# Last tiles of two batches side by side, loads in another order, and a new written-out order of steps, in an attention and Fourier-mixing kernel

## The chip, the cores and the metric

The kernel runs on one core of a Trainium2 chip. The metric is the device time of one execution in microseconds; runs of the same kernel are compared by their median. Engines are named as the profile names them: PE (TensorE), DVE (VectorE), ACT (ScalarE), POOL (GpSimd) and SP (SyncE, which here only issues DMAs). A "q" behind an engine's name is its issuing sequencer.

## The reference

There are 4 batches, 4 heads, 1088 positions and heads of 32, so d_model is 128. First comes a linear attention with a polynomial sketch, then a Fourier mix and a small network:

```python
a, b = x @ S1.T, x @ S2.T                 # r = 8 each
phi(x) = outer product of a and b         # 64 features
kv  = sum over s of phi(k) v ;  z = sum over s of phi(k)
att = phi(q) kv / (phi(q) z + 1e-6)       # heads side by side: 1088 x 128
u   = att + real(fft(fft(att, axis=seq), axis=d_model))
un  = (u - mean(u)) / sqrt(var(u) + 1e-6) # over d_model
out = u + relu(un @ w_ch1) @ w_ch2        # 128 -> 512 -> 128
```

## The kernel before

**Tiles.** 1088 rows of a batch are 8 full tiles of 128 rows and a rest of 64. The rests ("last tiles") of two batches share one tile of 128 partitions: `kes`, `ves` and `qes` hold them for k, v and q, with the first batch of a pair in partitions 0 to 63 and the second in 64 to 127. A pair's last tiles are loaded in pieces by `load_last` (L169, one load for each batch), `load_qe` (L186, two loads for each batch) and `load_q0` (L196, four loads of a single row for a pair).

**Chains and their letters.** The work is written as Python generators, one for each chain, and a string `ORDER` says in which order their steps are put down; a step lasts until the next `yield`. For batch b: `k` makes phi(k) and kv (transposes `ptrk` L378, copy `kT`, sketch products `pab` L387, `ak` and `kp` L395, the sums `pk` L409, `pkv` L420, copy `kvz`); `q` makes phi(q) transposed (`ptrq` L476, copy `qT`, `pq` L491, copies `qa`, products `qpT` L505); `v` copies v beside a column of ones (`vpad`, on POOL); `p` makes the attention's output (`pnd` L526, then `den`, `rec`, `x` on DVE, sums `xw` and `xf` on POOL); `z` is the sequence transform (`pz`, `pze`, and `zr` on POOL). `d` and `m` are the two halves of the network in a batch (`pT`, copy `uT`, `ph` L666, relu `ht` on ACT and DVE in turn, `po` L679, `ot` on DVE, output), and `D` and `M` the halves of u and its statistics (`pu`, `u`, `stats` on DVE, `mv` on POOL, `rstd` on ACT). `y`, `e`, `E` are the chains of a pair's last tiles: `y` transposes k's and q's last tile (`ptrE`), copies both (`eT`), multiplies (`pabE`, `ae`, `ep`) and transposes q's part back (`pqptE`, `qpTe`). `S` sets up constants and issues the loads of batch 0, `T` makes the tables of sines in four steps, `W` the weights, `L` issues the loads of one further batch.

**What sets the order.** There is no scheduler: each engine runs its instructions in the order in which `ORDER` puts them down, and waits on semaphores for what an instruction needs. The string `BANKS` says which of the eight PSUM banks each step takes; a step waits until the bank's last reader is done. Tiles in the pool `load` have three buffers. Loads and outputs go through SP's queue in the order written, but k's second half and k's last tiles for batch 0, which ACT issues. For batch 0 the queue order is half of k, half of q, q's last tiles, the other half of q, v, v's last tiles, q's single rows. Ten matmuls on zeros (`keep_warm`) stand at the start of PE.

Of the kernel before, what the change touches and what calls it, by code (L numbers as in the profile page):

```python
# [10 lines left out]
FP32 = mybir.dt.float32  # L11
# [20 lines left out]
def _back(ap, n):  # L32
# [7 lines left out]
S k0 T S k0 v0 q0 L k0 q0 q0 y0 q0 k0 q0 k0 q0 q0 y0 y0 k0 T k0 q0 q1 k1 k1 q1 k0 q0 y0  # L40
T k1 q0 k1 k1 q1 T q1 p0 p0 v1 L p0 q1 q1 p0 p0 k1 T p0 k1 q1 v2 q1 q2 q1 q2 k1 p0 q1 k2
k2 W y1 q2 p1 p0 p1 p1 p1 p1 p1 q2 y1 L p1 k2 q2 y1 z0 k3 z0 k3 v3 q3 z0 d0 q3 m0 q2 k2
q2 z0 k2 k2 k3 q2 k2 D0 z1 m0 q2 k3 q2 m0 d0 z1 y1 k3 z1 M0 d0 k2 m0 E0 e0 m0 q3 p2 M0
q3 k3 D0 E0 q3 M0 p2 p1 p2 p2 p2 q3 k3 q3 q3 p2 k3 m0 q3 m0 q3 d0 E0 z1 M1 p2 e0 D0 d0
d1 e0 p2 p3 p3 M1 p3 p3 p3 m1 p3 e0 p3 z2 e0 d0 m1 d0 m1 D1 z2 e0 e0 m1 d1 m1 D2 d1 d2
M1 p3 d1 m1 d2 D2 D1 d1 d2 z3 D1 z3 z2 m1 z2 d1 z3 d1 d2 d2 e1 E1 z3 M2 e1 E1 e1 e1 e1
d2 D2 m2 M2 d2 E1 e1 e1 M2 D3 m2 m2 m2 m2 M3 m3 m2 m3 D3 d3 M3 m2 D3 m3 m3 M3 m3 d3 d3
d3 d3 m3 m3 d3 m3 d3 d3
"""
BANKS = [  # L50
# [11 lines left out]
def kernel(  # L62
# [74 lines left out]
    s_n = const.tile([128, 4], FP32, name="s_n")  # L137
    tx = const.tile([128, NTAB], FP32, name="tx")
# [15 lines left out]
    xbz = [const.tile([128, DM], BF16, name=f"xbz{i}") for i in range(B)]  # L154
    kes = [const.tile([128, H, D], FP32, name=f"ke{i}") for i in range(2)]
# [13 lines left out]
    def load_last(eng, src, dst_e, b):  # L169
        p0 = E * (b % 2)  # L170
        eng.dma_start(
            dst_e[b // 2][p0 : p0 + E, :, :],
            bass.AP(tensor=src.tensor, offset=src.offset + (b * H * S + 1024) * D,
                    ap=[[D, E], [S * D, H], [1, D]]),
        )
# [10 lines left out]
    def load_qe(eng, b):  # L186

        for c in range(2):
            p0 = E * (b % 2) + 32 * c
            eng.dma_start(  # L190
                qes[b // 2][p0 : p0 + 32, :, :],
                bass.AP(tensor=q.tensor, offset=q.offset + (b * H * S + 256 + 544 * c) * D,
                        ap=[[D, 32], [S * D, H], [1, D]]),
            )

    def load_q0(eng, b):  # L196
        for c in range(2):
            p0 = E * (b % 2) + 32 * c
            eng.dma_start(
                qes[b // 2][p0 : p0 + 1, :, :],  # L200
                bass.AP(tensor=q.tensor, offset=q.offset + (b * H * S + 544 * c) * D,
                        ap=[[D, 1], [S * D, H], [1, D]]),
            )

    def loads(b):
        km[b] = load.tile([128, H, 8, D], FP32, name="km", tag="km")
        vm[b] = load.tile([128, H, 8, D], FP32, name="vm", tag="vm")
        qt[b] = load.tile([128, 2, H, 4, D], FP32, name="qt", tag="qt")
        if b == 0:
# [60 lines left out]
    def chain_start():  # L270
# [14 lines left out]
        for i in range(4):  # L285
            iota(s_f[32 * i : 32 * i + 32, 2:3], [[1, 1]], 256 + 544 * (i % 2), 1)
# [10 lines left out]
        for i, t_ in enumerate(vpads):  # L297
            nc.vector.memset(t_[:, 8, :, :], 0.0)
            nc.vector.memset(t_[:, 0:8, :, D : D + 1], 1.0)
            nc.vector.memset(t_[E * i : E * i + E, 8, :, D : D + 1], 1.0)  # L300
        for t_ in xbz:
            nc.vector.memset(t_[:], 0.0)
        for i in range(4):
            nc.vector.memset(s_f[32 * i : 32 * i + 1, 2:3], 544.0 * (i % 2))
        nc.vector.memset(kk[:, DM : DM + 1], 0.0)
        nc.vector.memset(kk[:, DM + 32 : DM + 33], 544.0)
        nc.vector.tensor_scalar(out=s_n[:, 0:3], in0=s_f[:, 0:3], scalar1=1.0 / S, scalar2=None,
# [63 lines left out]
    def chain_k(b):  # L371
# [32 lines left out]
        for hh in range(2):  # L404
            for t in range(NT):
                for h in (hh, hh + 2):
                    src = kp[:, h, t, :] if t < 8 else ep[:, 0, h, :]
# [19 lines left out]
    def chain_y(i):  # L427

        a = Y[i]
        eT = tT.tile([128, 2, 128], FP32, name="eT", tag="eT")  # L430
        ptr = bank("ptrE")
        nc.tensor.transpose(ptr[:, 0:128], kes[i][:, :, :], ident_f[:, :])
        nc.tensor.transpose(ptr[:, 128:256], qes[i][:, :, :], ident_f[:, :])
        nc.scalar.copy(eT[:, :, :], ptr[:, 0:256])
        yield
        pab = bank("pabE")
        for c in range(2):
            for j in range(2):
                nc.tensor.matmul(
                    pab[64 * j : 64 * j + 64, 64 * c : 64 * c + 64],  # L440
                    eT[:, c, 64 * j : 64 * j + 64], sblk[:, :, :], start=True, stop=True)
        a_e = abp.tile([128, 8, R], FP32, name="ae", tag="ae")
        nc.scalar.copy(a_e[:, :, :], _ap(pab, 0, 128, 0, [[16, 8], [1, R]]))
        yield
        ep = ppp.tile([128, 2, H, 64], FP32, name="ep", tag="ep", bufs=2)
        nc.vector.tensor_tensor(
            out=_ap(ep, 0, 128, 0, [[64, 8], [R, R], [1, R]]),
            in0=_ap(a_e, 0, 128, 0, [[R, 8], [1, R], [0, R]]),
            in1=_ap(pab, 0, 128, R, [[16, 8], [0, R], [1, R]]), op=MULT)
        a["ep"] = ep  # L450
        yield
        qpTe = qpTp.tile([128, 2, 128], FP32, name="qpTe", tag="qpTe")
        a["qpTe"] = qpTe
        pt = bank("pqptE")
        for pr in range(2):
            nc.tensor.transpose(pt[:, 128 * pr : 128 * pr + 128],
                                ep[:, 1, 2 * pr : 2 * pr + 2, :], ident_f[:, :])
        nc.scalar.copy(qpTe[:, :, :], pt[:, 0:256])
        yield

    def chain_v(b):
# [3 lines left out]
        r = slice(E * (b % 2), E * (b % 2) + E)  # L465
        nc.gpsimd.tensor_copy(vpad[r, 8, :, 0:D], ves[b // 2][r, :, :])
# [46 lines left out]
    def chain_p(b):  # L513
# [4 lines left out]
        for t0 in (0, 3, 6):  # L518
            pnd = bank("pnd")
            for t in range(t0, t0 + 3):  # L520
                for pr in range(2):
                    o = 132 * (t - t0) + 66 * pr
                    for j in range(2):
                        r = slice(64 * j, 64 * j + 64)
                        lhsT = qpT[:, t, pr, r] if t < 8 else Y[b // 2]["qpTe"][:, pr, r]
# [27 lines left out]
        r = slice(E * (b % 2), E * (b % 2) + E)  # L553
        nc.scalar.copy(xbz[b][r, :], x[r, 8, :])
# [5 lines left out]
    def chain_z(b):  # L560
# [30 lines left out]
        o = E * (b % 2)  # L591
        nc.scalar.copy(zes[b // 2][:, :, o : o + E], _ap(pze, 0, 128, 0, [[E, 2], [1, E]]))
# [7 lines left out]
    def chain_u(b, g):  # L600
# [22 lines left out]
        rstd = sp.tile([128, 4, 1], FP32, name="rstd", tag="rstd")  # L623
# [11 lines left out]
        nc.gpsimd.tensor_tensor(out=m, in0=m, in1=d, op=ADD)  # L635
        nc.scalar.activation(out=rstd[:, 0:nt, :], in_=m, func=ACT.Sqrt, bias=bias_eps[:, :],
# [5 lines left out]
    def chain_f(b, g):  # L642
# [53 lines left out]
        if g == 2:  # L696
            for j in range(4):
                o = out.offset + (2 * b * S + 544 * j) * DM
                nc.sync.dma_start(
                    bass.AP(tensor=out.tensor, offset=o + 257 * DM, ap=[[DM, 31], [1, DM]]),  # L700
                    ot[32 * j + 1 : 32 * j + 32, 0, :])
                nc.sync.dma_start(
                    bass.AP(tensor=out.tensor, offset=o, ap=[[DM, 1], [1, DM]]),
                    ot[32 * j : 32 * j + 1, 0, :])
# [20 lines left out]
    for b in range(2):  # L725
        chains[f"y{b}"] = (lambda b=b: chain_y(b))
        chains[f"e{b}"] = (lambda b=b: chain_f(b, 2))
# [40 lines left out]
```

## Time and profile before

| what | value |
|---|---|
| median of 3 runs | 99.22 us (98.99 to 100.25) |
| the profiled execution: time | 99.94 us |
| the profiled execution: span from first to last instruction | 97.2 us |
| mean granted TensorE clock | 0.993 |
| busy: PE, DVE, ACT, POOL | 83.0, 68.1, 62.3, 44.5 us |
| read from and written to device memory | 7.22 and 2.23 MB |

The span lies inside the profiled execution; 2.74 us are around it. Busy time of PE is modelled and counts overlapping matmuls once. In the views a row "line engine op out<-in xcount" is a group of like instructions, and brackets or "<-" name what ended the idle time before it.

### The profile page before, as it was taken

To read this page: it belongs to the slowest core of one execution; us is meant where nothing else is said; L and a number is where in the kernel's file an instruction comes from. 1 tells how busy PE (TensorE), PEld (TensorE's weight loads), DVE (VectorE), ACT (ScalarE), POOL (GpSimd) and SP (SyncE) were. 2 spreads that over 40 slices of the span, in tenths; PEclk is the share of its full clock that TensorE was granted. 3 is DMA by queue.
4 is the path that set the end of the run, shared out by engine and by line. 5 is a ranking of instruction groups with operands and counts; after the bars stand their busy time and mean duration, and the time that the engine had idled before them with its cause. 6 is when DMAs were issued, how large, how long until landed. Compare 5 with 4: busy or idle time off the path is not lost.

```text
span 97.2 us, 3683 instructions
## 1 busy us (share of the span) xinstructions
PE 83.0 (85%) x1486; PEld 63.8 (66%) x1486; DVE 68.1 (70%) x223; ACT 62.3 (64%) x154; POOL 44.5 (46%) x103
## 2 busy tenths in 40 slices
PE   5998548599899796899998998959999999999930
PEld 1357426497897365786986797849876789665630
DVE  5850567983997109990368698886986979599980
ACT  6008339476927985398289887786199987587700
POOL 7200050009930499999300058397389775506000
PEclk9999999999999999999999999999999999999997
DMA  2926729999446389600000000011003005130333
GB/s 37 260 51 143 233 37 282 254 338 283 67 117 163 86 251 210 195 8 0 10 0 7 0 7 0 7 47 61 0 7 117 18 0 169 56 109 24 114 103 113
DMA packets 15232, 9.67 MB, mean 100 GB/s; under 512 B 4080, under 2 KB 15088, under 8 KB 15216
## 3 DMA queue, kind: packets, MB, share of 16 engines
q1 hardware_dynamic: 14320, 9.12, 34.5%
q10 hardware_dynamic: 896, 0.34, 1.5%
q8 instruction: 11, 0.18, 0.8%
q14 instruction: 5, 0.04, 0.2%
HBM read 7.22 MB, written 2.23 MB: 97 GB/s over the span
## 4 chain that ended last, share of the span: by engine, by line
PE 33%; DMA 19%; DVE 16%; SPq 15%; issue 5%; POOL 5%; ACT 3%; DVEq 0%
DMA km<-in_k_dram 7%; PE ph L666 6%; SPq L181 6%; DMA vm<-in_v_dram 5%; DVE ot L687 5%; DMA qt<-in_q_dram 5%; PE pq L491 3%; PE pnd L526 3%; PE po L679 3%; DVE ht L671 3%; SPq L163 3%; PE pz L574 3%; DVE stats L625 3%; DVE qpT L505 2%; PE pab L387 2%
## 5 line engine op out<-in xcount | busy, mean ns | idle before, releaser
L505 DVE TENSOR_TENSOR qpT<-qa,pq 128x256 f32<-128x256 f32 x32 | 11.8, 417 | 6.3 <-ACT qa L498 6.3
L463 POOL COPY vpad<-vm 128x1024 f32<-128x1024 f32 x4 | 4.2, 1039 | 22.9 <-DMA vm<-in_v_dram 17.5
L395 DVE TENSOR_TENSOR kp<-ak,pab 128x1024 f32<-128x1024 f32 x8 | 9.6, 1216 | 6.1 <-ACT ak L391 4.3
L671 DVE TENSOR_SCALAR ht<-ph 128x512 bf16<-128x512 f32 (+1 forms) x20 | 11.6, 603 | 2.2 <-PE ph L666 2.2
L498 ACT COPY qa<-pq 128x256 f32<-128x256 f32 x32 | 10.2, 379 | 3.9 <-PE pq L491 3.4
L666 PE MATMUL ph<-uT,w_b 128*128 128x512 bf16 (+1 forms) x40 | 10.8, 347 | 1.6 <-DVE qpT L505 1.3
L549 POOL TENSOR_TENSOR xw<-x 128x512 f32<-128x512 f32 x8 | 10.0, 1272 | 2.4 <-PE pkv L420 1.5
L687 DVE SCALAR_TENSOR_TENSOR ot<-po,rstd,u 128x128 f32<-128x128 f32 x34 | 9.5, 345 | 1.6 <-DMA out_dram<-ot 1.0
L669 ACT ACTIVATE ht<-ph 128x512 bf16<-128x512 f32 (+1 forms) x20 | 10.1, 533 | 0.6 <-PE ph L666 0.5
L679 PE MATMUL po<-w_b,ht 128*128 128x128 bf16 x136 | 10.0, 220 | 0.5 <-ACT ht L669 0.2
L551 POOL TENSOR_TENSOR xf<-xw 128x512 bf16<-128x512 f32 x8 | 10.0, 1273 | 0.3
L631 POOL TENSOR_TENSOR mv<-stats 128x4 f32<-128x4 f32 (+1 forms) x10 | 2.0, 201 | 16.7 <-DVE stats L625 15.0
L679 PEld LDWEIGHTS <-ht 128*128 128x128 bf16 x136 | 8.2, 98 | 1.7 <-ACT ht L669 0.6
L491 PE MATMUL pq<-qT,sab 32*64 32x256 f32 x256 | 9.0, 387 | 0.4 <-DVE x L536 0.4
L526 PEld LDWEIGHTS pnd<-kvz,qpT 128*64 128x64 f32 x256 | 8.1, 137 | 1.6 <-issue 0.8
L526 PE MATMUL pnd<-kvz,qpT 128*64 128x66 f32 x256 | 8.8, 223 | 0.3 <-issue 0.3
L409 PE MATMUL pk<-kp,vpad 128*33 128x64 f32 x256 | 8.6, 219 | 0.0
L409 PEld LDWEIGHTS pk<-kp,vpad 128*33 128x33 f32 x256 | 7.8, 111 | 0.4 <-ACT uT L661 0.4
L381 ACT COPY kT<-ptrk 128x512 f32<-128x512 f32 x8 | 4.5, 596 | 5.3 <-PE ps L323 5.3
L536 DVE TENSOR_TENSOR x<-pnd,rec 128x384 f32<-128x384 f32 x12 | 6.7, 558 | 0.6
L625 DVE BATCH_NORM_STATS2 stats<-u 128x6 f32<-128x128 f32 x34 | 7.1, 278 | 0.0
L476 PE MATMUL ptrq<-ident_f,qt 128*128 128x128 f32 x32 | 4.9, 277 | 2.6 <-DMA qt<-in_q_dram 2.6
(144 smaller groups left out, 196.7 us busy)
## 6 DMA issues: line engine op xcount, KB each, us to landing
qt<-in_q_dram SPq DMA_DIRECT2D x16, 128.0 KB
vm<-in_v_dram SPq DMA_DIRECT2D x4, 512.0 KB
km<-in_k_dram SPq DMA_DIRECT2D x3, 512.0 KB
out_dram<-ot SPq DMA_DIRECT2D x6, 256.0 KB
w_f<-in_moe_w_ch_dram SPq DMA_DIRECT2D x2, 256.0 KB
out_dram<-ot SPq DMA_DIRECT2D x4, 128.0 KB
km<-in_k_dram SPq DMA_DIRECT2D x1, 256.0 KB
km<-in_k_dram ACTq DMA_DIRECT2D x1, 256.0 KB
```

The source lines that it names most:

```text
L409: nc.tensor.matmul(pk[p0 : p0 + D + 1, 64 * hh : 64 * hh + 64], vpad[:, t, h, :], src, start=(t == 0), stop=(t == NT - 1))
L491: nc.tensor.matmul(pq[t][64 * c : 64 * c + 64, 256 * ab : 256 * ab + 256], _ap(sab, 32 * r, 32, 64 * ab, [[1, 64]]), _ap(qT, 32 * r, 32, 5 ...
L498: nc.scalar.copy(qa[:, i, :], pq[i][:, 0:256])
L505: nc.vector.tensor_tensor(out=_ap(qpT, 0, 128, 1024 * g + 256 * (i % 2) + i // 2, [[128, 2], [512, 2], [2, 64]]), in0=_ap(qa, 0, 128, 256 ...
L526: nc.tensor.matmul(pnd[r, o : o + 66], lhsT, kv[:, pr, :, :], start=True, stop=True)
L549: nc.gpsimd.tensor_tensor(out=xw[:, i, :, :], in0=x[:, 0:4, :], in1=x[:, 4:8, :], op=f)
L625: nc.vector.bn_stats(stats[:, i, :], u[:, i, :])
L666: nc.tensor.matmul(ph[:, 0:n], w1_b[:, 128 * c : 128 * c + 128], uT[:, 0:n], start=True, stop=True)
L669: nc.scalar.activation(out=ht[:, c, 0:n], in_=ph[:, 0:n], func=ACT.Relu)
L671: nc.vector.tensor_relu(ht[:, c, 0:n], ph[:, 0:n])
L679: nc.tensor.matmul(po[:, (i - i0) * DM : (i - i0 + 1) * DM], ht[:, c, i * 128 : (i + 1) * 128], w2_b[:, c, :], start=(c == 0), stop=(c == 3))
L687: nc.vector.scalar_tensor_tensor(out=ot[:, i, :], in0=po[:, (i - i0) * DM : (i - i0 + 1) * DM], scalar=rstd[:, i, :], in1=u[:, i, :], op0= ...
```

## The change

Six things change.

1. A pair's last tiles lie interleaved: row r of the pair's first and second batch stand in partitions 2r and 2r+1. One `load_last` with a pattern over both batches then brings k's tile, one v's, two q's, and two the single rows of q. v's tile is multiplied by `par`, a column of 0 and 1 that keeps one batch of the two, `qpTes` holds zeros in the other batch's columns, and the outputs of a last tile go out in four DMAs for a pair instead of eight.
2. The loads stand in another order: k (in two halves), q, v, and then the last tiles of a pair; the single rows of q come with the second batch. ACT issues only S1 and S2.
3. q's last tile gets a chain of its own, `w`; `y` keeps k's. The body of both is `last_tile`.
4. In `D`, `M` and `E` the square root for `rstd` becomes a step of its own, so that it can be placed later than POOL's `mv`.
5. The constants follow: `par`, `s_n` for the interleaved rows, no zeroing of `xbz` and of the whole last tile of `vpad`.
6. `ORDER` and `BANKS` are replaced whole. The first two table steps now stand ahead of the first k step; before, the first stood behind it and the second after most of batch 0's steps.

```diff
-S k0 T S k0 v0 q0 L k0 q0 q0 y0 q0 k0 q0 k0 q0 q0 y0 y0 k0 T k0 q0 q1 k1 k1 q1 k0 q0 y0
-T k1 q0 k1 k1 q1 T q1 p0 p0 v1 L p0 q1 q1 p0 p0 k1 T p0 k1 q1 v2 q1 q2 q1 q2 k1 p0 q1 k2
...
+S T T k0 S k0 q0 k0 q0 q0 k0 y0 q0 L q0 k0 y0 v0 y0 q0 q0 k0 q0 k1 k1 L T q0 L k0 k1 k0
+q1 k1 q0 q1 w0 p0 q1 q1 k1 v1 q1 p0 p0 k1 T k1 w0 p0 k2 q2 q1 w0 k2 T k1 w0 q1 q1 p0 q1
+p0 v2 k2 p1 q1 k2 q2 y1 k2 W p0 q2 y1 p1 p1 y1 k2 p1 q2 p0 k2 p1 k3 k3 z0 q2 k2 w1 q2 z0
...
+    qpTes = [const.tile([128, 2, 128], FP32, name=f"qpTe{i}") for i in range(2)]
...
-    def load_last(eng, src, dst_e, b):
-        p0 = E * (b % 2)
+    def load_last(eng, src, dst, i, r0, n, p0):
         eng.dma_start(
-            dst_e[b // 2][p0 : p0 + E, :, :],
-            bass.AP(tensor=src.tensor, offset=src.offset + (b * H * S + 1024) * D,
-                    ap=[[D, E], [S * D, H], [1, D]]),
+            dst[p0 : p0 + 2 * n, :, :],
+            bass.AP(tensor=src.tensor, offset=src.offset + (2 * i * H * S + r0) * D,
+                    ap=[[D, n], [H * S * D, 2], [S * D, H], [1, D]]),
         )
...
+        load_rows8(nc.sync, k, km[b], b, 0, 2)
         if b == 0:
-            load_rows8(nc.sync, k, km[0], 0, 0, 2)
...
-            load_rows8(nc.scalar, k, km[0], 0, 2, 4)
-            for i in (0, 1):
-                load_last(nc.scalar, k, kes, i)
-        else:
-            load_rows8(nc.sync, k, km[b], b)
-            if b == 2:
-                for i in (2, 3):
-                    load_last(nc.sync, k, kes, i)
+        load_rows8(nc.sync, k, km[b], b, 2, 4)
         load_q(nc.sync, b, 0)
-        if b % 2 == 0:
-            for i in (b, b + 1):
-                load_qe(nc.sync, i)
         load_q(nc.sync, b, 1)
         load_rows8(nc.sync, v, vm[b], b)
         if b % 2 == 0:
-            for i in (b, b + 1):
-                load_last(nc.sync, v, ves, i)
-            for i in (b, b + 1):
-                load_q0(nc.sync, i)
+            load_last(nc.sync, k, kes[i], i, 1024, E, 0)
+            load_last(nc.sync, v, ves[i], i, 1024, E, 0)
+            for c in range(2):
+                load_last(nc.sync, q, qes[i], i, 256 + 544 * c, 32, 64 * c)
+        else:
+            for c in range(2):
+                load_last(nc.sync, q, qes[i], i, 544 * c, 1, 64 * c)
...
-            nc.vector.memset(t_[:, 8, :, :], 0.0)
...
-        for t_ in xbz:
+        for t_ in qpTes:
             nc.vector.memset(t_[:], 0.0)
...
+        nc.vector.tensor_scalar(out=odd_i[:, :], in0=odd_i[:, :], scalar1=1, scalar2=None, op0=AND)
+        nc.vector.tensor_copy(par[:, 1:2], odd_i[:, :])
...
+    def last_tile(src):
+        eT = tT.tile([128, 128], FP32, name="eT", tag="eT")
+        ptr = bank("ptrE")
+        nc.tensor.transpose(ptr[:, 0:128], src[:, :, :], ident_f[:, :])
+        nc.scalar.copy(eT[:, :], ptr[:, 0:128])
+        yield
+        pab = bank("pabE")
+        for j in range(2):
+            nc.tensor.matmul(
+                pab[64 * j : 64 * j + 64, 0:64],
+                eT[:, 64 * j : 64 * j + 64], sblk[:, :, :], start=True, stop=True)
+        a_e = abp.tile([128, 4, R], FP32, name="ae", tag="ae")
+        nc.scalar.copy(a_e[:, :, :], _ap(pab, 0, 128, 0, [[16, 4], [1, R]]))
+        yield
+        ep = ppp.tile([128, H, 64], FP32, name="ep", tag="ep", bufs=3)
+        nc.vector.tensor_tensor(
+            out=_ap(ep, 0, 128, 0, [[64, 4], [R, R], [1, R]]),
+            in0=_ap(a_e, 0, 128, 0, [[R, 4], [1, R], [0, R]]),
+            in1=_ap(pab, 0, 128, R, [[16, 4], [0, R], [1, R]]), op=MULT)
+        return ep
...
     def chain_y(i):
+        Y[i]["ep"] = yield from last_tile(kes[i])
+        yield
+
+    def chain_w(i):
+        ep = yield from last_tile(qes[i])
+        yield
         pt = bank("pqptE")
...
-        nc.scalar.copy(qpTe[:, :, :], pt[:, 0:256])
+        for j in range(2):
+            nc.scalar.copy(_ap(qpTes[j], 0, 128, j, [[128, 2], [2, 64]]),
+                           _ap(pt, 0, 128, j, [[128, 2], [2, 64]]))
...
-        r = slice(E * (b % 2), E * (b % 2) + E)
-        nc.gpsimd.tensor_copy(vpad[r, 8, :, 0:D], ves[b // 2][r, :, :])
+        nc.gpsimd.tensor_scalar(out=vpad[:, 8, :, 0:D], in0=ves[b // 2][:, :, :],
+                                scalar1=par[:, b % 2 : b % 2 + 1], scalar2=None, op0=MULT)
...
         nc.gpsimd.tensor_tensor(out=m, in0=m, in1=d, op=ADD)
+        yield
+        rstd = sp.tile([128, 4, 1], FP32, name="rstd", tag="rstd")
         nc.scalar.activation(out=rstd[:, 0:nt, :], in_=m, func=ACT.Sqrt, bias=bias_eps[:, :],
...
-            for j in range(4):
-                o = out.offset + (2 * b * S + 544 * j) * DM
+            for c in range(2):
+                for r0, n, p0 in ((257, 31, 2), (0, 1, 0)):
...
```

More of the change, by code (lines that the diff above doesn't have):

```diff
@@ L137 @@
     s_n = const.tile([128, 4], FP32, name="s_n")
+    odd_i = const.tile([128, 1], I32, name="odd_i")
+    par = const.tile([128, 2], FP32, name="par")
     tx = const.tile([128, NTAB], FP32, name="tx")
@@ L284, in chain_start @@
         iota(kk[:, DM + E : DM + 320], [[1, 2], [2, 128]], 1, 0)
-        for i in range(4):
-            iota(s_f[32 * i : 32 * i + 32, 2:3], [[1, 1]], 256 + 544 * (i % 2), 1)
+        nc.gpsimd.iota(odd_i[:, :], pattern=[[1, 1]], base=0, channel_multiplier=1)
+        iota(s_f[0:64, 2:3], [[1, 1]], 512, 1)
+        iota(s_f[64:128, 2:3], [[1, 1]], 1600, 1)
         iota(kk[:, DM + 320 :], [[1, 2], [2, 128]], 545, 0)
@@ L425, in chain_k, with chain_y @@
                            _ap(pkv, 64 * c, 64, 0, [[D + 1, 2], [1, D + 1]]))
-    def chain_y(i):
-        a = Y[i]
-        eT = tT.tile([128, 2, 128], FP32, name="eT", tag="eT")
+    def last_tile(src):
+        eT = tT.tile([128, 128], FP32, name="eT", tag="eT")
         ptr = bank("ptrE")
-        nc.tensor.transpose(ptr[:, 0:128], kes[i][:, :, :], ident_f[:, :])
-        nc.tensor.transpose(ptr[:, 128:256], qes[i][:, :, :], ident_f[:, :])
-        nc.scalar.copy(eT[:, :, :], ptr[:, 0:256])
+        nc.tensor.transpose(ptr[:, 0:128], src[:, :, :], ident_f[:, :])
+        nc.scalar.copy(eT[:, :], ptr[:, 0:128])
         yield
         pab = bank("pabE")
[L437 to L443, printed above, removed]
+        for j in range(2):
[4 more added lines that the diff above has]
+        nc.scalar.copy(a_e[:, :, :], _ap(pab, 0, 128, 0, [[16, 4], [1, R]]))
         yield
-        ep = ppp.tile([128, 2, H, 64], FP32, name="ep", tag="ep", bufs=2)
+        ep = ppp.tile([128, H, 64], FP32, name="ep", tag="ep", bufs=3)
         nc.vector.tensor_tensor(
[L447 to L450, printed above, removed]
+            out=_ap(ep, 0, 128, 0, [[64, 4], [R, R], [1, R]]),
+            in0=_ap(a_e, 0, 128, 0, [[R, 4], [1, R], [0, R]]),
+            in1=_ap(pab, 0, 128, R, [[16, 4], [0, R], [1, R]]), op=MULT)
+        return ep
+    def chain_y(i):
+        Y[i]["ep"] = yield from last_tile(kes[i])
         yield
-        qpTe = qpTp.tile([128, 2, 128], FP32, name="qpTe", tag="qpTe")
-        a["qpTe"] = qpTe
+    def chain_w(i):
+        ep = yield from last_tile(qes[i])
+        yield
         pt = bank("pqptE")
@@ L524, in chain_p @@
                         r = slice(64 * j, 64 * j + 64)
-                        lhsT = qpT[:, t, pr, r] if t < 8 else Y[b // 2]["qpTe"][:, pr, r]
+                        lhsT = qpT[:, t, pr, r] if t < 8 else qpTes[b % 2][:, pr, r]
                         nc.tensor.matmul(pnd[r, o : o + 66], lhsT, kv[:, pr, :, :],
@@ L552, in chain_p @@
                                     op=f)
-        r = slice(E * (b % 2), E * (b % 2) + E)
-        nc.scalar.copy(xbz[b][r, :], x[r, 8, :])
+        nc.scalar.copy(xbz[b][:, :], x[:, 8, :])
         yield
@@ L590, in chain_z @@
                         start=False, stop=(par == 1 and t == 1))
-        o = E * (b % 2)
-        nc.scalar.copy(zes[b // 2][:, :, o : o + E], _ap(pze, 0, 128, 0, [[E, 2], [1, E]]))
+        nc.scalar.copy(_ap(zes[b // 2], 0, 128, b % 2, [[128, 2], [2, E]]),
+                       _ap(pze, 0, 128, 0, [[E, 2], [1, E]]))
         yield
@@ L622, in chain_u @@
         mv = sp.tile([128, 3, 4], FP32, name="mv", tag="mv")
-        rstd = sp.tile([128, 4, 1], FP32, name="rstd", tag="rstd")
         for i in range(nt):
```

61 lines of the change are left out of this document (25 added, 36 removed), and 14 rows, old and new, of the table BANKS.

## The prediction

> **What bounds the kernel now.** I read the page first.
>
> ```profile
> span 97.2 us, 3683 instructions
> ...
> PE 83.0 (85%) x1486; PEld 63.8 (66%) x1486; DVE 68.1 (70%) x223; ACT 62.3 (64%) x154; POOL 44.5 (46%) x103
> ...
> PE   5998548599899796899998998959999999999930
> ...
> PE 33%; DMA 19%; DVE 16%; SPq 15%; issue 5%; POOL 5%; ACT 3%; DVEq 0%
> ```
>
> TensorE is the busiest engine, but its gaps lie in the first half, and in the chain that ended last a third of the span is DMA and its issuing on SP (19% + 15%). The busy time by stage says how much. I cut at 5.44 (first real transpose, after the ten warm-up matmuls), at 43.44 (first pT matmul, where the second half of the network starts), and at 93.41 (last matmul):
>
> ```profile
> 5.44:43.44 38.00, 31.29 (x656) 25.12 (x654) 24.45 (x55) 24.04 (x63) 16.67 (x23) 1.00 0.67 171
> 43.44:93.41 49.97, 47.48 (x828) 37.08 (x824) 38.48 (x128) 36.78 (x91) 25.53 (x65) 1.00 0.11 37
> 93.41:97.20 3.79, 0.00 (x0) 0.00 (x0) 1.11 (x5) 0.00 (x0) 0.00 (x0) 0.82 0.42 138
> ```
>
> The first numbers are length and PE busy. So the span is 5.44 + (31.29 work + 6.71 idle) + (47.48 + 2.49) + 3.79 = 97.2 us, and two thirds of the idle time is in the stage that loads. PE's timeline names most of those 6.71 us, in brackets:
>
> ```profile
> 10.87 0.63 PE L476 MATMUL ptrq<-ident_f,qt 128*128 128x128 f32 x4 [1.43 <-DMA qt<-in_q_dram]
> 14.03 0.30 PE L433 MATMUL ptrE<-ident_f,qe 128*128 128x128 f32 x1 [1.23 <-DMA qe<-in_q_dram]
> 19.56 0.63 PE L476 MATMUL ptrq<-ident_f,qt 128*128 128x128 f32 x4 [1.13 <-DMA qt<-in_q_dram]
> 34.21 0.30 PE L433 MATMUL ptrE<-ident_f,qe 128*128 128x128 f32 x1 [0.45 <-DMA qe<-in_q_dram]
> 39.27 0.39 PE L439 MATMUL pabE<-sblk,eT 128*64 128x64 f32 x6 [1.33 <-issue]
> ```
>
> The first four, 4.24 us, wait for loads; 0.46 more (pk after ep at 17.12) follows from the late qe. The load queue shows why:
>
> ```profile
> 2.64 4.08 SPq L190 DMA_DIRECT2D qe<-in_q_dram  x4
> 6.77 1.26 SPq L181 DMA_DIRECT2D qt<-in_q_dram  x2
> 8.08 0.60 SPq L163 DMA_DIRECT2D vm<-in_v_dram  x1
> 8.72 1.26 SPq L171 DMA_DIRECT2D ve<-in_v_dram  x2
> 10.03 2.62 SPq L199 DMA_DIRECT2D qe<-in_q_dram  x4
> 12.70 0.44 SPq L163 DMA_DIRECT2D km<-in_k_dram  x1
> ```
>
> Each issue takes some 0.65 us of SP, whatever it brings: four qe loads (64 KB in all) hold the second half of q until 6.77, four single rows (2 KB) cost 2.62 us, and k of the second batch goes out only at 12.70. In the program every load also waits for the one eight before it. The data path is not the limit, as stretches of the same load stage show (last numbers: DMA share, GB/s):
>
> ```profile
> 12.20:14.60 2.40, 1.17 (x34) 0.58 (x26) 1.59 (x3) 0.88 (x3) 1.27 (x2) 1.00 0.27 36
> 14.60:17.00 2.40, 2.06 (x72) 1.48 (x56) 1.76 (x5) 2.20 (x8) 0.00 (x0) 1.00 0.96 284
> 19.40:21.90 2.50, 2.34 (x20) 2.20 (x20) 2.10 (x4) 1.94 (x5) 0.00 (x0) 1.00 1.08 336
> 24.30:26.70 2.40, 2.11 (x70) 2.02 (x68) 2.33 (x5) 2.40 (x5) 2.20 (x7) 1.00 0.43 68
> ```
>
> Large loads run at 254 to 336 GB/s (I take 285); where last tiles and single rows are issued it is 36 to 68.
>
> **The change, part by part.**
>
> **Loads.** Ahead of k of the second batch stand 11 loads on SP instead of 16: 0.72 + 11 x 0.65 = 7.9 us instead of 12.70. Now the data path decides. k, q and v of batch 0 are 1.57 MB: from 1.9 us at 285 GB/s until 7.4. The last tiles of a pair keep their 128-byte pieces; 196 KB at 36 to 68 GB/s is 2.9 to 5.4 us; 3.8 taken, nearer the faster row since fewer issues thin it out: ke at 8.7, all at 11.2. Then 1.84 us for each 0.52 MB: k1 13.0, q1 14.9, v1 16.7, weights 18.5, k2 20.3, q2 22.1, v2 24.0, last tiles 27.8, the rest by 33.3 (now 41). When are they wanted? pab ends at 9.6 (9.45 now); then ptrq 0.45, pq 1.05, ptrE 0.25, a wait of 0.65 (below), pabE 0.3, a wait of 0.3, pq 1.05 and half of pk 1.0 make 14.6 for k1. Going on in PE's new order in the same way gives 17.7 for q1, 24 to 25 for k2 and q2, 30 for the second ke: no load is late. So 4.24 + 0.46 us of idle time go. If the path were slower, see the last rival.
>
> The Trainium skill ("DMA: Bandwidth & Descriptors", Specifications) says that transfers under 512 B stay below line rate. It speaks against this change: the pieces stay at 128 B, and now they stand in one block ahead of the next batch. The 36 to 68 GB/s above agree; if all of that were packets and not issuing, a pair would cost 5.4 us, and k1 would land at 14.6, just when it is wanted.
>
> **The front.** ACT no longer issues ke (6.03 to 7.42, which held the first kT copy to 7.46), but the first two sines now stand there (1.15 us, as at 16.13 to 17.28) and wait for DVE's angles, now done at 6.2. DVE's constants lose about 1.2 us (four xbz memsets 0.33, vpad 0.42, four single rows 0.42) and gain about 1.4 (two qpTe memsets at 0.27, by wdummy's row of the same size, and nine operations on a column or less at 0.07 to 0.1). kT comes 0.2 later: **+0.2**. Behind it wait sblk's products and all of batch 0.
>
> **Own steps and splits.** The k and q halves of the last tile are now apart: eT four copies of 128x128 at 0.26 (u's row) instead of two at 0.38, +0.3; ae two more at 0.2; qpTe four at 0.26 (its strided form is not in the trace: 0.26 to 0.38) instead of two at 0.38, +0.3; together +1.0 on ACT, which is idle for 14 of the 38 us. ep four at about 0.4 for two at 0.69: +0.2 on DVE. ve's copy becomes a product, 0.54 (center's row) for 0.29: +1.0 on POOL, which now waits 10.10 us for v. None is charged to the end; uncovered, they cost at most 2.2. Eight output issues fewer on SP: nothing, since SP waits there (27.7 us for its first). rstd as its own step frees ACT from some of its 5.1 us of waiting for POOL; it still waits for the same five small POOL operations, only placed later.
>
> **New waits in the first stage.** (1) pabE needs eT, which ACT copies behind two qa copies: 0.65, with pq's second half queued behind it on PE. (2) That pq needs banks that DVE frees after kp and two qpT: 0.3. (3) DVE now does the second tables (3.25 us, 17.55 to 20.8 before) ahead of batch 0's second qpT group, and batch 1's first pq takes a bank of it: 20.3 against 19.5, 0.8, with pnd, pk and the copies behind. (4) The 1.33 of "issue" has no releaser in the trace: 0 to 1.33, I take 0.65, the middle. With the front, 2.6 us instead of 6.71. Ends: 0.5 if ACT's and DVE's turns fall well, 6.7 if all comes back.
>
> **Second stage.** PE's new order puts 4.3 us of batch 2 and 3 (pab 0.93, pk 2.1, pq 1.05, pnd 0.75, pkv 0.17, less ptrq 0.44 and pze 0.27) ahead of the first pT. 43.2 us of PE remain there; DVE keeps 37.9 of its 39.6 (38.48 + 1.11; a qpT pair, 0.7, and an x group, 0.95, move ahead with them): 88% of PE's time instead of 83%. Less slack: 2.8 instead of 2.49. Ends: 0.5, and 6.2 if DVE keeps all its 11.5 us of gaps up to its last operation (37.9 + 11.5 - 43.2).
>
> **Sum.** 5.44 + 78.77 + 2.6 + 2.8 + 3.79 = 93.4 us of span, 3.8 less. The profiled execution took 99.94 us, 2.74 more than its span, and lies 0.72 above the median of 99.22. So the new median is 99.22 - 3.8 = **95.4 us**.
>
> **The rivals.**
>
> *PE packs better.* "Busy" holds hidden waits: 16 po matmuls take 1.06 us in mid-stage, but two late groups took 1.15 and 1.40 and the closing 32 took 2.60, so 0.09 + 0.34 + 0.48 = 0.9 us over. If these go and the stalls shrink from 5.4 to 3.5: 95.4 - 0.9 - 1.9 = 92.6. Against it: the closing group waits for ht on DVE and ACT, as it will again.
>
> The skill ("Perfetto Trace Analysis", Identifying the Most-Contended Engine) calls matmul busy time a poor measure and takes weight-load time instead: 37.08 of 49.97 us in the second stage. This speaks for that rival; by it 12.9 us would be room, not 2.5.
>
> *DVE takes over.* The gain of the first stage is given back: second-stage stalls of 6.2, so 95.4 + 3.4 = 98.8, no difference. For it: at 65.03 PE stood 1.00 us for qpT; normalisation, relu and outputs all queue on one in-order DVE. Against it: with later data DVE sat idle for 13.6 us in the first stage, and kept PE waiting little in the second.
>
> *The loads run no faster: slower than before.* All of a pair's last tiles now precede k of the next batch, so if the path, not the issuing, set the early pace, everything behind is late. Place: q2, wanted by PE at 29.97 in the old run, with 4.9 MB up to it. Turning point: 4.9 MB / (29.97 - 0.7) = 167 GB/s. At 150 q2 lands at 33.4, 3.4 us late: 99.2 + 3.4 = 102.6. For it: the load stage averages 171. Against: 284 and 336 in the rows above, with the dips where small loads are issued.
>
> **How the numbers follow.** Forecast 0.55; better packing 0.17; DVE 0.18; slow loads 0.10. A measurement here tells about 2%, 97.2 to 101.2. Faster: 0.55 + 0.17 = 0.72; the same 0.18; slower 0.10. The ends of the unknown stalls alone give 91.0 to 102.9; 92.5 to 99.0 leaves out the slow loads and about a tenth beside.
>
> **What would show it.** Right: no wait of PE for qt or qe over 0.3 us; k of batch 1 issued near 8 us and the last load landed by about 34; PE idle in front of the first pT under 3 us; the ends of the last matmul and the span still 3.8 apart. Wrong: a DMA row among PE's longest releasers (slow loads); more than 4 us of PE idle after the first pT (DVE); PE standing over 1 us for a bank behind DVE's tables.

## The result, and the profile after

| kernel | median | the kernel before beside it | ratio, 95% interval |
|---|---|---|---|
| changed | 90.92 us (90.52 to 92.69) | 99.73 us | 0.9125 [0.9039, 0.9211] |
| changed, again on a later chip | 91.81 us (90.56 to 92.79) | 99.41 us | 0.9194 [0.9126, 0.9261] |

Some executions of a kernel come out one to three per cent longer than its others; the medians are over all executions, and the ratios with an interval leave the long ones out.

The forecast was 95.4 us, 92.5 to 99.0. The sign was right; the gain, 8.8 us beside 3.8, is more than twice the forecast, and the time lies below the range. The profiled execution took 90.52 us, 1.82 more than its span. Its page, in the order of the lines shown of before:

```profile
span 88.7 us, 3662 instructions
...
PE 80.2 (90%) x1481; PEld 63.0 (71%) x1486; DVE 67.7 (76%) x223; ACT 62.3 (70%) x160; POOL 45.7 (52%) x102
...
PE   4998979999999999999999999999999999798700
...
PE 64%; DVE 21%; ACT 4%; DMA 3%; issue 2%; SPq 1%; DVEq 0%; ACTq 0%
```

PE has nines from slice 7 on where it had holes up to the middle, and in the chain that ended last DMA and SP's issuing fell from 19% + 15% to 3% + 1%: PE itself is the chain now. The stretches, cut as before at the first transpose, the first pT matmul and the last matmul:

```profile
5.11:40.94 35.83, 34.62 (x804) 28.36 (x802) 25.88 (x62) 26.24 (x74) 18.13 (x23) 1.00 0.68 181
40.94:84.08 43.14, 41.72 (x672) 33.14 (x674) 36.85 (x123) 34.57 (x84) 25.43 (x65) 1.00 0.12 42
84.08:88.70 4.62, 0.01 (x1) 0.00 (x0) 1.12 (x4) 0.00 (x0) 0.00 (x0) 0.78 0.33 115
```

So 5.11 + (34.62 work + 1.21 idle) + (41.72 + 1.42) + 4.62 = 88.7. Against the forecast span of 93.4: start -0.33, PE's work 76.34 instead of 78.77 (-2.43), first-stage stalls 1.21 instead of 2.6 (-1.39), second-stage stalls 1.42 instead of 2.8 (-1.38), tail 4.62 instead of 3.79 (+0.83). Together -4.7.

What is left of PE's brackets in the first stage is two rows, and none is a load:

```profile
7.68 1.34 PE L374 MATMUL pab<-sblk,kT 128*64 128x64 f32 x32 [0.44 <-ACT kT L368]
11.58 0.34 PE L423 MATMUL pabE<-sblk,eT 128*64 128x64 f32 x4 [0.67 <-ACT eT L419]
```

The load queue:

```profile
1.73 2.75 SPq L184 DMA_DIRECT2D qt<-in_q_dram  x4
...
6.51 1.29 SPq L174 DMA_DIRECT2D qe<-in_q_dram  x2
7.85 1.11 SPq L166 DMA_DIRECT2D km<-in_k_dram  x2
```

q goes out whole by 4.5 us, its last tiles in two issues instead of four, and k of the second batch at 7.85 instead of 12.70; the last load packet ends at 33.1.

### The profile page after: what moved, and what is told of

The parts are those of the page before. It is cut to its first block, busy times and chain, and to the rows that moved or that the text cites. A ratio compares the mean times of both kernels' runs of the same rounds, so it can differ in the third digit from the quotient of the medians.

```text
span 88.7 us, 3662 instructions
## 1 busy us (share of the span) xinstructions
PE 80.2 (90%) x1481; PEld 63.0 (71%) x1486; DVE 67.7 (76%) x223; ACT 62.3 (70%) x160; POOL 45.7 (52%) x102
## 4 chain that ended last, share of the span: by engine, by line
PE 64%; DVE 21%; ACT 4%; DMA 3%; issue 2%; SPq 1%; DVEq 0%; ACTq 0%
PE pnd L518 11%; PE pq L483 10%; PE pk L396 10%; DVE ot L679 6%; DVE ht L663 5%; PE pab L374 5%; DVE stats L615 4%; PE ptrq L468 4%; PE ptrk L365 3%; DMA out_dram<-ot 3%; PE ph L658 3%; PE pz L565 3%; PE po L671 2%; PE pT L650 2%; PE pz L558 2%
## 5 line engine op out<-in xcount | busy, mean ns | idle before, releaser
L671 PE MATMUL po<-w_b,ht 128*128 128x128 bf16 x136 | 9.4, 219 | 0.4 <-ACT ht L661 0.4
L518 PE MATMUL pnd<-kvz,qpT 128*64 128x66 f32 x256 | 9.4, 224 | 0.0
L610 ACT COPY u<-pu 128x512 f32<-128x512 f32 (+1 forms) x10 | 5.3, 526 | 2.2 <-PE pu L605 0.8
L483 PEld LDWEIGHTS pq<-qT,sab 32*64 32x64 f32 x256 | 4.9, 131 | 2.3 <-PE ptrE L418 0.8
```

What stands on the lines that cost most here:

```text
L483: nc.tensor.matmul(pq[t][64 * c : 64 * c + 64, 256 * ab : 256 * ab + 256], _ap(sab, 32 * r, 32, 64 * ab, [[1, 64]]), _ap(qT, 32 * r, 32, 5 ...
L518: nc.tensor.matmul(pnd[r, o : o + 66], lhsT, kv[:, pr, :, :], start=True, stop=True)
L671: nc.tensor.matmul(po[:, (i - i0) * DM : (i - i0 + 1) * DM], ht[:, c, i * 128 : (i + 1) * 128], w2_b[:, c, :], start=(c == 0), stop=(c == 3))
```

## The experiments

The medians, each beside the kernel before on the same chip. "Joint" and "own" say whether the square root for rstd follows POOL's mv in the same step or is a step of its own. All runs but e6 and e13 keep the interleaved layout of the last tiles, with its constants and its four output DMAs for a pair.

| run | loads of last tiles | order of steps | rstd | median | before |
|---|---|---|---|---|---|
| e1 | few, new places | old | joint | 100.38 | 99.89 |
| e2 | many, old places | new | own | 94.17 | 99.89 |
| e3 | as changed, second sines late | new | own | 90.66 | 99.89 |
| e4 | as changed | new | joint, early | 104.63 | 99.89 |
| e5 | few, old places | old | joint | 95.26 | 99.51 |
| e6 | many, old places | old | own | 100.03 | 99.51 |
| e10 | many, new places | new | own | 94.93 | 99.51 |
| e11 | few, old places | new | own | 91.86 | 99.51 |
| e9 | as changed | new | joint, late | 104.88 | 99.41 |
| e8 | as changed, 3 output buffers | new | own | 89.77 | 99.41 |
| e12 | the changed kernel again | new | own | 91.81 | 99.41 |
| e13 | the kernel before, warm-up cut small | old | joint | 97.43 (one run) | 99.41 |

**New loads under the old order (e1).** All of the new loads and constants; `ORDER`, `BANKS`, the joint chain `y` and the joint square root as before.

```diff
-S T T k0 S k0 q0 k0 q0 q0 k0 y0 q0 L ...
+S k0 T S k0 v0 q0 L k0 q0 q0 y0 q0 k0 ...
-    def chain_w(i):
```

> The loads, the interleaved layout and its constants as in the changed kernel; ORDER, BANKS, the joint chain for k's and q's last tile and the joint rstd step as before. Theory A (the loads held PE, the new order only follows them): PE's four waits for loads and the wait for ep go, 4.7 us in brackets and some 0.17 us of drained pipeline with each, the other waits stay: span 91 to 92.5 us, PE idle in front of the first pT under 2.5 us. Theory B (the order is what holds PE; early data find it waiting for ACT and DVE instead): span 94 us or more, with new waits of PE for ACT or DVE ahead of the first pT.

Ratio 1.0104 [0.9991, 1.0218]. One row of PE's timeline tells why:

```profile
16.72 0.45 PE L420 MATMUL ptrE<-ident_f,qe 128*128 128x128 f32 x1 [5.71 <-DMA qe<-in_q_dram]
```

The joint chain transposes q's last tile right after k's, and q's single rows, which belong to that tile, now come with batch 1's loads. What the few loads gave went into that one wait. Neither theory has this: the time is theory B's, but the wait is for a load. So q's own chain is no tidying: under the old order, with the joint chain, the new places of the loads gain nothing.

**Few loads in the old places, old order (e5).** To keep e1's collision out, the few loads stand where the many stood.

```diff
+        if b % 2 == 0:
+            load_last(nc.sync, k, kes[i], i, 1024, E, 0)
         load_q(nc.sync, b, 0)
+        if b % 2 == 0:
+            for c in range(2):
+                load_last(nc.sync, q, qes[i], i, 256 + 544 * c, 32, 64 * c)
         load_q(nc.sync, b, 1)
         load_rows8(nc.sync, v, vm[b], b)
+        if b % 2 == 0:
+            load_last(nc.sync, v, ves[i], i, 1024, E, 0)
+            for c in range(2):
+                load_last(nc.sync, q, qes[i], i, 544 * c, 1, 64 * c)
```

> The kernel before, with its old order of steps, its joint chain for both last tiles and its joint rstd, but with the interleaved last tiles brought by few loads, which stand where the old loads stood in the queue (single rows of q ahead of batch 1's k, not with batch 1 as in the first run). Theory (the issuing of many small loads made PE wait for q): q's second half is issued near 4.9 us instead of 6.77, q's last tiles 1.3 to 2 us earlier, batch 1's k near 8 instead of 12.70; the stalls of 1.43, 1.23, 1.13 and 0.45 us go or shrink to under 1 us in all, the stages behind them start some 3 to 4 us earlier, and the ratio to before is 0.955 to 0.975 (95 to 97 us). Rival (the old order was fitted to the late loads, so the stalls only change their place): PE idle stays over 7.5 us in all and the ratio is 0.985 or more.

95.26 against 99.51 us: 4.25 us less, ratio of the medians 0.957, what the first theory said. The size is loose: the seven times of the kernel before run from 97.51 to 100.77, and its two shortest (97.51 and 98.5) beside the three shortest here (94.71 to 95.38) give 2.9 us. (The profile is of an execution of 96.86 us, so of its rows mainly the releasers are used.) PE's timeline:

```profile
12.10 1.12 PE L478 MATMUL pq<-qT,sab 32*64 32x256 f32 x32 [0.73 <-DVE qpT L492]
14.96 0.31 PE L396 MATMUL pk<-ep,vpad 128*33 128x64 f32 x4 [0.46 <-DVE ep L433]
20.15 0.44 PE L441 MATMUL pqptE<-ident_f,ep 128*128 128x128 f32 x2 [1.65 <-DVE qpT L492]
...
36.17 0.39 PE L426 MATMUL pabE<-sblk,eT 128*64 128x64 f32 x6 [0.93 <-issue]
...
61.94 0.45 PE L652 MATMUL ph<-uT,w_b 128*128 128x128 bf16 x2 [0.99 <-DVE qpT L492]
```

No load is among the releasers. What remains is the stall without a releaser, and PE behind DVE, in three of these rows for a tile that the matmul doesn't read, so for the bank; none of these rows is left in the changed kernel. This is what the order is worth. The last was there in the kernel before too, with one more of its kind:

```profile
60.77 1.12 PE L491 MATMUL pq<-qT,sab 32*64 32x256 f32 x32 [0.36 <-DVE x L536]
65.03 0.45 PE L666 MATMUL ph<-uT,w_b 128*128 128x128 bf16 x2 [1.00 <-DVE qpT L505]
```

**Old loads under the new order (e2).** The changed kernel with as many loads as before, in the old places and on the old engines; ACT issues k's.

```diff
-            load_last(nc.sync, k, kes[i], i, 1024, E, 0)
+            for h in range(2):
+                load_last(nc.scalar, k, kes[i], i, 1024 + 32 * h, 32, 64 * h)
...
```

> The changed kernel with the loads as before in number, order and issuing engine (k's second half and k's last tiles of the first pair on ACT, two to four small loads for each last tile, four single rows), in the interleaved layout. Theory A: the new order wants k and q of batch 1 at 14 and 18 us, and they land at 16 to 21, so PE waits for DMA 4 to 7 us in sum ahead of the first pT: span 93 to 96 us. Theory B: the order finds other work, waits for DMA stay under 2 us: span below 91 us.

94.17 us, 0.9493 [0.9389, 0.9597]. PE's timeline:

```profile
8.95 1.34 PE L383 MATMUL pab<-sblk,kT 128*64 128x64 f32 x32 [1.75 <-ACT kT L377]
11.29 1.09 PE L477 MATMUL ptrq<-ident_f,qt 128*128 128x128 f32 x4 [0.99 <-DMA qt<-in_q_dram]
```

Both stalls are the loads' doing: ACT is held by issuing ke (and now also by the first sines), and q's second half is late. They are 2.3 us more than the 0.44 in the changed kernel, of the 2.4 to 3.3 us between the medians. Neither theory holds whole: PE waits for loads under 2 us, as B said, but the span is 92.6, not under 91. The order alone, on the old loads, is worth some 5 us by the ratio (4.0 to 6.1), 5.7 by the medians.

**As many loads as before, in the new places (e10); few loads in the old places (e11).** Both under the new order.

e10 cuts every load of a last tile in two; e11's queue is that of e5.

```diff
-            load_last(nc.sync, v, ves[i], i, 1024, E, 0)
+            for h in range(2):
+                load_last(nc.sync, v, ves[i], i, 1024 + 32 * h, 32, 64 * h)
...
```

```diff
         load_rows8(nc.sync, k, km[b], b, 2, 4)
+        if b % 2 == 0:
+            load_last(nc.sync, k, kes[i], i, 1024, E, 0)
         load_q(nc.sync, b, 0)
...
```

> The changed kernel with every load of a last tile cut in two (k, v, q's tiles and q's single rows: 6 more issues for a pair ahead of or in batch 1's loads, 12 in all), same bytes, same pieces of 128 bytes, same order. Theory (the issues, 0.65 us each on one queue, set the pace of the early loads): batch 1's k is issued near 10.5 us instead of 7.85, which its transpose at 14.3 still forgives, but q's single rows go out near 18.5 instead of 14.5 and PE, which wants them at 18.5, waits 1 to 2.5 us for them; 92 to 93.5 us, ratio 0.925 to 0.945. Rival (the packets, not the issues, decide): landing times and the time stay as in the changed kernel, 90.5 to 91.3 us.

> The changed kernel, few loads and new order of steps, but the few loads stand in the queue where the old ones stood: k's last tiles ahead of q, q's last tiles between q's halves, and q's single rows ahead of batch 1's k. Theory (the number of issues matters more than their order): q's second half is issued 2 us later than in the changed kernel and PE waits 0.3 to 1.2 us for it at its first transposes; all else is in time: 91 to 92.2 us. Rival (order of need carries what the loads bring): PE waits 2 us or more for q, and the time comes near the 94.17 us of the changed kernel with the old loads.

e10 took 94.93 us, 3 to 4 more than the changed kernel, and more than either theory said; e11 91.86, level with the upper of the changed kernel's two medians (no changed kernel ran beside these two). So under the new order the number of issues carries the loads' part, and their places are worth under 1 us. The wait of 0.3 to 1.2 us for q that e11's theory named did not come; no load is among its releasers. The first theory of e10 had the sign but not the place: q's single rows went out late, and PE stood 0.87 us at their transpose (the profile names a bank behind DVE there), yet the longest wait was for q of batch 2, which all the issues ahead push back to 21.15 us, where the changed kernel has it at 16.34 (PE's timeline, e10):

```profile
27.13 0.63 PE L474 MATMUL ptrq<-ident_f,qt 128*128 128x128 f32 x4 [1.47 <-DMA qt<-in_q_dram]
```

**The square root: own step or joint (e4, e9, e6).** e4 puts it back behind mv in the early step; e9 moves statistics, mv and square root together to the late step; e6 gives the kernel before an own step at the head of the next.

```diff
         nc.gpsimd.tensor_tensor(out=m, in0=m, in1=d, op=ADD)
-        yield
         rstd = sp.tile([128, 4, 1], FP32, name="rstd", tag="rstd")
         nc.scalar.activation(out=rstd[:, 0:nt, :], in_=m, func=ACT.Sqrt, bias=bias_eps[:, :],
                              scale=1.0 / DM)
+        yield
```

```diff
+        yield
         stats = sp.tile([128, 4, 6], FP32, name="stats", tag="stats")
...
-        yield
         rstd = sp.tile([128, 4, 1], FP32, name="rstd", tag="rstd")
```

```diff
+        yield
         nc.scalar.activation(out=rstd[:, 0:nt, :], in_=m, func=ACT.Sqrt, bias=bias_eps[:, :],
                              scale=1.0 / DM)
-        yield
         nc.vector.reciprocal(rstd[:, 0:nt, :], rstd[:, 0:nt, :])
```

> The changed kernel with the square root for rstd back in the step of the statistics, so that ACT's queue stands for POOL as before; order otherwise the same. If the own step is worth something, ACT's waits for POOL grow from 2.2 us to 5 us or more and the span by 0.5 to 2 us. If ACT has room in the second stage (34.6 of 43.1 us busy), the span stays within 0.3 us.

> The changed kernel, but the statistics (bn_stats on DVE, mv on POOL) are moved behind the new yield as well, so that statistics, mv and the square root all stand together at the later place that the order gives to the square root. Theory (what counts is the distance between POOL's mv and the square root on ACT, in which ACT does other things): ACT waits for POOL 10 us or more again and the time is 100 us or more, like the run with the joint step at the early place (104.6). Rival (the joint step was only too early for ACT in that order; a late place is enough): 91 to 94 us.

> The kernel before, with one edit: the square root for rstd stands at the head of the following step, behind whatever the order puts in between, and not behind the statistics in the same step. Loads and the order of everything else as before. Theory (the square root ahead of other ACT work costs only where the order packs ACT tightly): ACT's 5.1 us of waiting for POOL shrink to under 3, but PE's idle time in the second half was only 2.49 us, so the ratio is 0.985 to 1.01. Rival (the own step is worth several us by itself): ratio under 0.975, with the 1.00 and 0.36 us stalls of PE in the second half gone.

104.63 (1.046 [1.0273, 1.0647]), 104.88 (1.0549 [1.0454, 1.0644]) and 100.03 us. ACT's waits (total, times, longest), first of the changed kernel, then of e4; e9 has 14.9 us in 8:

```profile
ACT rstd L628 <- POOL mv L625: 2.2, 3, 1.3
```

```profile
ACT rstd L627 <- POOL mv L625: 13.6, 10, 2.3
```

Early or late, a square root that stands right behind mv stops ACT, and with it copies and relus that PE waits for, as in this row of e4's PE timeline:

```profile
50.94 1.38 PE L483 MATMUL pq<-qT,sab 32*64 32x256 f32 x26 [1.89 <-ACT ht L661]
```

What counts is the distance. In the old order the same edit shortened ACT's wait from 5.1 to 1.3 us and gave nothing: there PE was not held by it. The own step is worth nothing alone, and some 13 us inside this order.

**The second sines later (e3).** The forecast charged 0.2 us for two sines ahead of the first kT copy, and the bracket of 0.44 above seems to confirm it.

```diff
-S T T k0 S k0 q0 k0 q0 q0 k0 y0 q0 L q0 k0 y0 v0
+S T k0 S k0 q0 k0 q0 q0 k0 y0 q0 L q0 k0 y0 T v0
```

> The changed kernel with the second table step (the first two sines on ACT) moved from ahead of the first kT copy to behind the first ae copy; nothing else. If the sines ahead of kT cost what PE's wait of 0.44 us for kT shows, the span falls by 0.3 to 0.5 us. If they are hidden, or cost as much behind ae, where two qa copies then queue behind 1.15 us of sines, the span stays within 0.3 us or grows by up to 1 us.

90.66 us: no difference. The bracket at kT is gone from this trace, but the edit doesn't explain that: the first transposes start late here, at 5.45 us, and e8, e9 and e10, which start as late with the sines in their changed place, show no bracket either. So the median shows no cost of the sines, and the trace adds nothing to that.

**Three output buffers (e8), and the changed kernel again (e12).** In the changed kernel the last row of DVE is

```profile
84.87 1.12 DVE L679 SCALAR_TENSOR_TENSOR ot<-po,rstd,u 128x128 f32<-128x128 f32 x4 [0.98 <-DMA out_dram<-ot]
```

so the last outputs wait until an earlier output's transfer has read the buffer.

```diff
-    op = ctx.enter_context(tc.tile_pool(name="op", bufs=2))
+    op = ctx.enter_context(tc.tile_pool(name="op", bufs=3))
```

> The changed kernel with three buffers instead of two in the pool of output tiles. Theory (the last ot waits 0.98 us until the DMA of the output before the last has read its buffer, and that wait stands on the path to the end): the tail from the last matmul to the end of the span shrinks from 4.62 to 3.7 us and the time by 0.7 to 1.0 us against the changed kernel itself in this call. Rival (the last output's DMA is queued behind the ones before it on SP anyway): the tail stays over 4.3 us and the times are within 0.3 us of each other.

> The changed kernel as it is, to stand beside the run with three output buffers on the same chip: 90.5 to 91.5 us.

89.77 us, 0.9023 [0.8968, 0.9078], beside 91.81 (0.9194 [0.9126, 0.9261]) for the changed kernel on the same chip, itself 0.3 above what was expected of it: a version that beats both. The stretch from the last matmul to the end in e8:

```profile
84.21:87.80 3.59, 0.00 (x0) 0.00 (x0) 0.84 (x4) 0.00 (x0) 0.00 (x0) 0.70 0.43 148
```

DVE makes its last six ot in a row, 83.44 to 85.05, and the tail is 3.59 us. That is 1.03 less than 4.62; the gain of 2.0 (1.7 by the ratios) was larger than the 0.7 to 1.0 expected. Part of the rest is PE: its idle time in the second stage is 0.70 instead of 1.17 in e12's trace, where it stands 0.23 and 0.32 us at 76.3 and 76.9, and DVE 0.94 ahead of an `ot` at 75.08. The profile puts that wait of DVE down to ph; that it goes with the third buffer speaks for the buffer. What is left was not followed.

**The stall without a releaser (e13).** Forty warm-up matmuls of 128 columns instead of ten of 512, in the kernel before.

```diff
-        for i in range(n):
-            nc.tensor.matmul(warm[:, :], wdummy[:, 0:128], wdummy[:, :], ...)
+        for i in range(4 * n):
+            nc.tensor.matmul(warm[:, 0:128], wdummy[:, 0:128], wdummy[:, 0:128], ...)
```

> The kernel before with its ten warm-up matmuls of 512 columns cut into forty of 128: the same columns, but 60 instructions more at the start of TensorE's program (30 matmuls, 30 weight loads). It is to say what the 1.33 us without a releaser at pabE is, between two of eight matmuls that stand in a row with no wait between them. Theory (TensorE's program ran dry: a 16 KB packet of another DMA queue landed at 37.98, 0.05 us after the stall began, and 1.29 before it ended): the boundary comes some 60 instructions earlier in the program, so the stall leaves pabE: it stands in the pnd matmuls ahead of it, or is gone. Rival (something of pabE itself): a stall of 0.9 to 1.7 us stays between pabE's second and third matmul.

PE's timeline, where the kernel before had 1.33 us of "issue" inside this group, e5 0.93 and e6 1.61:

```profile
37.41 0.40 PE L439 MATMUL pabE<-sblk,eT 128*64 128x64 f32 x8
```

All eight run through. Nothing about pabE was changed; only the place of its instructions in TensorE's program moved by 60. But the place alone doesn't decide: in e1, whose TensorE instructions stand in the same order as e5's, they run through as well, at 42.26 us where e5's began at 34.96:

```profile
42.26 0.40 PE L426 MATMUL pabE<-sblk,eT 128*64 128x64 f32 x8
```

e13 was executed once, so the stall's going is shown, and its price in the median is not; up to 40.15, soon behind the group, PE stands 0.83 us for POOL's xf, a wait that the kernel before doesn't have there.

## Why the prediction was right or wrong, point by point

**Loads: the mechanism right, the size near it.** 11 issues put k1 out at 7.9 (7.85), the last load lands at 33.3 (33.1), and the four waits for q go. e5 measures this part under the old order, layout and constants included: 4.25 us between the medians, 2.9 between the shortest runs, where the prediction's waits for loads summed to 4.24. The closeness of the medians is luck, since e5 gained a bank wait of 1.65 and lost part of the "issue". One term was mis-sized, the 3.8 us for a pair's last tiles, from stretches with 36 to 68 GB/s. The changed kernel's stretch that is made of them (1119 of the packets that ended in it have 128 bytes, 19 have 1024):

```profile
8.00:9.00 1.00, 1.00 (x31) 0.83 (x25) 0.00 (x0) 0.77 (x2) 0.30 (x1) 1.00 0.96 154
```

154 GB/s, so 196 KB would take 1.3 us. The slow stretches of before were slow by issuing, as far as this rate and e10 tell: with twice the issues the same microsecond of e10 holds 753 of these packets. The Trainium skill's rule ("DMA: Bandwidth & Descriptors", Specifications) that pieces under 512 B miss line rate agrees: 154 against 254 to 336 for the large ones. But it decided nothing: e10, with the same bytes in the same pieces and twice the issues, lost 3 us or more.

**The order: the step that failed.** The new order was priced only by what it adds: four new waits, a moved front, less slack in the second stage. It was never asked which of the old stalls it removes apart from the loads. In the sum this made three terms too high: PE's work at 78.77, the stalls at 2.6 and at 2.8, which came to 76.34, 1.21 and 1.42. e2 has the order at some 5 us on the old loads; on the few loads it is 95.26 to 90.92 or 91.81, so 3.4 to 4.3. With the loads' 4.25 this makes the whole gain of 7.6 to 8.8, as it must, since e5 stands between the two kernels.

**New waits in the first stage: 2.6 against 1.21.** (1) eT: 0.65 predicted, 0.67 measured, in every run under the new order but e2 (0.54). (2) and (3), 0.3 and 0.8 for banks behind DVE, did not come: DVE's second tables ran from 13.91 to 17.2, well ahead of batch 1's pq at 19.57. The prediction had moved their old duration into the new order without placing their start. (4) Half of the 1.33 without a releaser: it is gone. By e13 and e1 it hangs on where in TensorE's program the group stands and on when PE gets there. Zero was one of its ends.

**The front: +0.2 against -0.33.** The prediction's own figures (angles at 6.2, then 1.15 of sines, so 7.35 against 7.46) had kT earlier, not later; it started at 7.06. The -0.33 is not the change's doing. The first transpose stands right behind the ten warm-up matmuls, with no wait between, and these took from 3.62 to 4.45 us in the traces of the new order, so that it started anywhere from 4.66 to 5.45 us; e8, e9 and e10 start at 5.44 as the kernel before did. In the changed kernel, then in the kernel before:

```profile
1.20 4.07 PE L246 MATMUL warm<-wdummy 128*128 128x512 bf16 x10 [1.20 <-DVE wdummy L251]
5.11 0.60 PE L365 MATMUL ptrk<-ident_f,km 128*128 128x128 f32 x4
```

```profile
1.20 4.45 PE L267 MATMUL warm<-wdummy 128*128 128x512 bf16 x10 [1.20 <-DVE wdummy L272]
5.44 1.06 PE L378 MATMUL ptrk<-ident_f,km 128*128 128x128 f32 x4
```

The same matmuls start 0.43 us apart at first and 0.22 apart from a moment on that differs between executions; why was not followed.

**Second stage: 2.8 of stalls against 1.42.** "Less slack" was an argument from shares, DVE at 88% of PE's time instead of 83%. The share came out as forecast (36.85 of 41.72), and yet the 1.00 and 0.36 behind DVE are gone. So they were not a matter of its load alone; that they hung on what stood ahead in its queue fits, and was not tested by itself.

**PE's work taken over unchanged: 78.77 against 76.34.** The rival *PE packs better* named this: hidden waits in "busy", 0.9 us in po. From start to start, po's matmuls take 8.22 us, 0.38 of them visible idle, where the kernel before has 9.38 with 0.63: 0.9 less, as the rival said. Another 0.8 is no gain of the order: the first transposes and ps took 1.04 us (5.11 to 6.15) where they had taken 1.82 (5.44 to 7.26), with the warm-up matmuls' pace above. In e12's trace the work is 77.2, in e8's 77.3, so the term was 1.5 to 2.4 too high; what po and the first transposes leave of it was not followed. The Trainium skill's warning ("Perfetto Trace Analysis", Identifying the Most-Contended Engine) that matmul busy time is a poor measure agrees with the trace; its weight-load room of 12.9 us in the second stage is now 43.14 - 33.14 = 10.0.

**Own steps charged at nothing: right alone, wrong as a description.** e6 shows no gain from it, e4 and e9 show that the order rests on it. A part that costs and brings nothing by itself can still be the one without which the others lose 13 us.

**Tail: 3.79 against 4.62.** The prediction carried it over unasked; the new order brings the last three outputs closer together, and two buffers no longer suffice (e8).

**The rivals.** *PE packs better*, 92.6 at a chance of 0.17, came nearest, and the result went beyond it: it kept stalls of 3.5, and they are 2.63. *DVE takes over* and *the loads run no faster* are refuted by the rows above: no DMA among PE's releasers, 1.4 us of idle after the first pT. The signs set down for being right held but for the tail. The range's lower end took one rival's figure for the floor, though the bounds of the stalls alone gave 91.0, and PE's work, with no lower bound of its own, stood in it as fixed.

## What to carry to other kernels

When a written-out order is replaced, price it by the old stalls that it could remove, each with its releaser, and not only by the waits that it may add; a sum that takes busy time over unchanged leaves out what stands hidden in it, and needs a lower end for that. On a queue that issues many small loads, count the issues first: here 0.6 to 0.65 us each, and twice as many for the same bytes cost 3 us or more of some 91. Keep a step apart from the slow producer that it waits for, and after a change that packs the end closer look at the buffers of the outputs.

## What the runs showed of the hardware that was not expected

TensorE can stand for 0.93 to 1.61 us between two matmuls that wait for nothing the profile shows. In three of the five traces of the old order (before, e5, e6) the stall sat between pabE's second and third matmul, and ended 1.27 to 1.42 us after a 16 KB packet of the queue that the page calls "q8 instruction" (ends at 37.98, 34.90, 38.12; the stall's at 39.27, 36.17, 39.54). In all five it is the fourth such packet. In e1, with the same order of TensorE's instructions as e5, and in e13, with 60 instructions more ahead of it, the group runs through: there the fourth packet ended at 37.17 and 31.16, 5 to 6 us before the group began (42.26 and 37.41). The Trainium skill ("Runtime: NRT & Kernel Launch", Instruction fetch mechanics) says that the program is fetched in blocks of 16 KiB and that crossing a boundary is mostly hidden: the packets' size agrees, and by these times one crossing was not hidden. That this is the cause is argued from the times, not shown. Why the packet came late in three traces is open; most of the eleven or twelve in each trace are followed by no stall.
